# Block-sparse attention and a low-rank mixer with MLP: another order of the first loads and mask products, and other constants of the planner

## The chip, the core and the metric

The kernel runs on one core of a Trainium2 chip. The core has a matrix engine (TensorE, PE in the profile; its weight loads are shown as PEld), a vector engine (VectorE, DVE), a scalar engine for activation functions (ScalarE, ACT), a general-purpose engine (GpSimd, POOL) and an engine that mostly issues transfers (SyncE, SP). Each runs its own instructions in order, and they wait for each other on semaphores. ScalarE, SyncE and GpSimd also issue transfers (DMAs); all of them share 16 DMA engines.

The metric is the device time of one execution in microseconds (us). Smaller is better.

## What is computed

For 4 batches, 8 heads, 768 positions and a head width of 64, attention is taken under a mask of 24 x 24 blocks of 32 positions. The result, 768 x 512 per batch, is mixed along the positions by a product of rank 32, added to itself, and goes through a two-layer MLP of width 2048. Cut to its core:

```python
scores = scale * np.matmul(q, k.transpose(0, 1, 3, 2))
mask = np.abs(blk_i - blk_j) <= 1
mask = mask | (blk_i == 0) | (blk_j == 0) | (blk_i == n_blocks - 1) | (blk_j == n_blocks - 1)
for qb in range(n_blocks):
    for kb in sampled_blocks[qb]:
        mask[qb * 32:(qb + 1) * 32, kb * 32:(kb + 1) * 32] = True
scores = np.where(mask, scores, -1000000000.0)
attn = softmax(scores)
x = (attn @ v)                      # heads side by side: (B, S, 512)
u = x + (x.T @ U @ V).T             # rank 32, along the positions
out = u + np.maximum(u @ w_ch1, 0.0) @ w_ch2
```

Three random blocks per block row (sampled_blocks) come in as data; the rest of the mask is fixed and known when the program is built.

## The kernel before

**Tiling.** Two heads make a pair; there are 16 pairs, 4 per batch. A pair has 9 units. A unit is one tile of scores (psc, 128 keys x 512 queries for both heads, or two key tiles x 256 queries), two to four matmuls, one exponential of 128 x 1024 on ScalarE (est, line 497), and later its share of the value products (pav).

**Two stages.** In the first stage, pairs 0 to 3 run in a fixed order: scores of a unit, then the value products of the unit three before it, then side work listed in at_unit (line 983). Here the mask is added inside the score product: the upper or lower half of the rows of qa holds a mask row per query (0 or -240), and that of ka holds one-hot rows that pick the key's block. So the first scores need, for both heads, the turned (transposed) queries and keys and these extra rows. From the second stage on (pairs 4 to 15, batches 1 to 3) the mask is a product with 0/1 tiles m01 on VectorE (line 518), and the units are interleaved with the MLP of the batch before.

**The planner.** The order of the second stage is made when the program is built. A clock per engine (clk) is advanced by estimated costs, for example 0.92 us for an exponential and us=0.0315 for a value product (line 581). The MLP's steps lie in a list, fill, each with a cost: 0.65 us for a first-layer step (w1), 0.434 for a second-layer step (w2). Every fill step that is emitted adds its cost times a weight to a credit (line 1223: 0.87 for w1 steps, 1.13 for w2 steps). A unit that is due is emitted if the credit reaches rate() (line 1184), that is, the fill left less 12.5 us (14.5 in the last such batch), divided by the units left. It is also held back when ScalarE's clock is ahead of TensorE's by over 0.5 us (line 1195). If no fill step can go, a unit may go without credit. A first-layer or second-layer tile is made in two phases, which use the two halves of the array's rows crosswise; between them (the "swap" steps) 0.2 us must pass, which a unit may fill. Before the next batch's MLP opens, its last turned input (uT) must be there.

**The start.** The path to the first exponential is this:

- VectorE clears zeros, small, ka's extra rows, cbd, Ut and Vt (lines 286 to 292).
- SyncE loads sampled_blocks (sbi), then the queries in two parts (qld), the second part of the keys, and one set of one-hot rows. ScalarE's queue loads the first part of the keys (line 308), the fixed pattern (small, line 309, whose memory lies in w1t, which is its name in the profile), the identity id16 and the other set of one-hot rows. small has 24 rows: one-hot columns, the fixed mask, and block numbers.
- GpSimd writes ones into vt, then copies one element from kld into vld (line 321), which makes SyncE's load of v and all behind it wait for the first keys.
- TensorE runs eight products on zeros (warm_pe).
- VectorE compares block numbers with sbi (eq), reduces (cb) and joins the fixed mask (cbd), lines 336 to 359.
- TensorE makes three mask products (mask_mm: pm0 and pm1 for the first 512 queries of each head, pm2 for the other 256), one more warm product, turns four query tiles and two key tiles (turn_some, lines 410 and 411), and runs four more warm products.
- The first queries are cast by VectorE and the first keys by ScalarE (lines 403, 404). mask_rows turns pm0 and pm1 into extra rows of qa, on VectorE and ScalarE. half_copy puts the turned tiles into qa (VectorE) and ka (ScalarE).
- Then the first scores follow. pm2's rows and the rest of the turns follow after the first unit (lines 988 to 995).

Of the kernel before, what the change touches and what calls it, by code (L numbers as in the profile page):

```python
# [11 lines left out]
FP16 = mybir.dt.float16  # L12
# [5 lines left out]
P = 128  # L18
# [3 lines left out]
def kernel(  # L22
# [12 lines left out]
    nc = tc.nc  # L35

    B, H, S, D = q.shape
    BLK = 32
    NB = S // BLK
    T = S // P  # L40
# [7 lines left out]
    QA = 512  # L48
    QB = S - QA
# [16 lines left out]
    small_np = np.concatenate(  # L66
        [oh_np[:NB], ms_np, np.tile(np.arange(NB, dtype=np.float16), (NB, 1))], axis=1
    )
    eye16_np = np.eye(P, dtype=np.float16)

    small_dr = nc.inline_tensor(small_np, name="small_const")
# [6 lines left out]
    stpool = ctx.enter_context(tc.tile_pool(name="stpool", bufs=2))  # L78
# [19 lines left out]
    keep = tc.keep_in_program_order  # L98
# [5 lines left out]
    clk = {"pe": 0.0, "act": 0.0, "dve": 0.0, "pool": 0.0}  # L104
# [5 lines left out]
    def pst_tile(shape, dtype, name, tag):  # L110
        n = singles[tag][0]
        singles[tag].rotate(1)
        return psp[tag].tile(shape, dtype, tag=f"{tag}{n}", name=name)
# [58 lines left out]
    def mm(out, lhsT, rhs, start, stop, loose=False, us=0.0):  # L172
        clk["pe"] += us
        ins = nc.tensor.matmul(  # L174
            out, lhsT, rhs, start=start, stop=stop, skip_group_check=loose
        )
        keep(ins)
        return ins
# [25 lines left out]
    vts = [consts.tile([P, H, T, DV], FP16, name=f"vt{i}") for i in range(2)]  # L204
    Ut = wpool.tile([P, T, P], FP16)
    Vt = wpool.tile([P, T, P], FP16)
    Vd = wpool.tile([P, T, P], FP16)
    w1t = wpool.tile([P, NCC, CH], FP16)
    small = w1t[:, 0, 0 : S + 2 * NB]
    w2t = wpool.tile([P, NJJ, HD], FP16)  # L210

    rows = [slice(0, D), slice(D, P)]
# [12 lines left out]
    def new_ld(i, nm):  # L225
        lds[i, nm] = ldpool.tile([P, 2, T, D], FP32, tag="ld" + nm, name=nm + "ld")
        return lds[i, nm]
# [56 lines left out]


    keep(nc.vector.memset(zeros, 0.0))
    keep(nc.vector.memset(small, 0.0))
    for h in (1, 0):
        keep(nc.vector.memset(ka[0][h][mrows[h], :], 0.0))
    keep(nc.vector.memset(cbd, 0.0))  # L290
    keep(nc.vector.memset(Ut, 0.0))
    keep(nc.vector.memset(Vt, 0.0))
    qld, kld = new_ld(0, "q"), new_ld(0, "k")
    TQ, TK = 4, 2
    q0, k0 = src_of("q", 0), src_of("k", 0)

    def hot_rows(eng, st, h, n):
        r0 = mrows[h].start
        keep(eng.dma_start(out=ka[st][h][r0 : r0 + n, :], in_=oh_dr.ap()[0:n]))
# [3 lines left out]
            out=sbi[0:NB].rearrange("z r w -> z (r w)"),  # L303
            in_=sampled_blocks.bitcast(I32),
        )
    )
    keep(nc.sync.dma_start(out=qld[:, :, 0:TQ], in_=q0[:, :, 0:TQ]))
    keep(nc.scalar.dma_start(out=kld[:, :, 0:TK], in_=k0[:, :, 0:TK]))
    keep(nc.scalar.dma_start(out=small[0:NB], in_=small_dr.ap()))
    keep(nc.sync.dma_start(out=qld[:, :, TQ:T], in_=q0[:, :, TQ:T]))  # L310
    keep(nc.scalar.dma_start(out=id16, in_=eye16_dr.ap()))
    keep(nc.sync.dma_start(out=kld[:, :, TK:T], in_=k0[:, :, TK:T]))
    hot_rows(nc.scalar, 0, 0, NB)
    hot_rows(nc.sync, 0, 1, NB)
    keep(nc.scalar.activation(out=dummy, in_=zeros[:, 0:1], func=AF.Exp))


    for vt in vts:
        keep(nc.gpsimd.memset(vt[:, :, :, D : D + 1], 1.0))
    vld = new_ld(0, "v")  # L320
    keep(nc.gpsimd.tensor_copy(out=vld[:, 0, 0, 0:1], in_=kld[:, 0, 0, 0:1]))
    keep(nc.sync.dma_start(out=vld, in_=src_of("v", 0)))
# [4 lines left out]
    def warm_pe(n):  # L327
        for _ in range(n):
            mm(
                warm.rearrange("p (r n) -> p r n", r=4), zeros,  # L330
                zeros[:, None, :].broadcast_to([P, 4, P]), True, True,
            )

    warm_pe(8)

    keep(
        nc.vector.tensor_tensor(
            out=eq[0:NB],
# [7 lines left out]
            out=cb[0:NB],  # L346
            in_=eq[0:NB].rearrange("z r c -> z c r"),
# [6 lines left out]
            out=cbd[0:NB, :, 0:NB],  # L354
# [2 lines left out]
            op=ALU.max,  # L357
        )
    )
    qst = stpool.tile([P, T, 2, D], FP16, tag="stq", name="qst")  # L360
    kst = stpool.tile([P, T, 2, D], FP16, tag="stk", name="kst")

    def cast0(eng, st, ld, t0, t1):
        keep(
            eng(
                out=st.rearrange("p t h d -> p h t d")[:, :, t0:t1],
                in_=ld[:, :, t0:t1],
            )
        )


    def mask_mm(o, a, e):
        mm(
            o,
            cbd.rearrange("z a c -> z (a c)"),
            small[:, a:e],
            True, True,
        )

    def mask_rows(eng, h, i, a, e):  # L380
        o = qa[0][h][mrows[h], a:e]
        if eng == "dve":
            keep(
                nc.vector.tensor_scalar(
                    out=o, in0=i[mrows[h]],
                    scalar1=-MASK_BIAS, scalar2=MASK_BIAS, op0=ALU.mult, op1=ALU.add,
                )
            )
        else:
            keep(  # L390
                nc.scalar.activation(
                    out=o, in_=i[mrows[h]],
                    func=AF.Copy, scale=-MASK_BIAS, bias=MASK_BIAS,
                )
            )
# [3 lines left out]
    pm2 = pscp.tile([P, 2, 512], FP32, tag="double1", name="pm")  # L399
    mask_mm(pm0[:, 0, 0:QA], 0, QA)  # L400
    mask_mm(pm1, 0, QA)
    mask_mm(pm2[:, 0, 0:QB], QA, S)
    cast0(nc.vector.tensor_copy, qst, qld, 0, TQ)
    cast0(nc.scalar.copy, kst, kld, 0, TK)
    mask_rows("dve", 0, pm0[:, 0, 0:QA], 0, QA)
    mask_rows("act", 1, pm1, 0, QA)
    warm_pe(1)
    pq = pst_tile([P, T, P], FP16, "pturn", tag="ps")
    pk = pst_tile([P, T, P], FP16, "pturn", tag="ps")
    turn_some(qst, pq, 0, TQ)  # L410
    turn_some(kst, pk, 0, TK)
    warm_pe(4)

    def half_copy(eng, dst, h, pt, t0, t1):
        keep(
# [105 lines left out]
    def weights(ests, g, j, h):  # L521

        tr, kind = divmod(g, 2)
        if j < 4:
            return ests[3 * tr + kind][:, h, j * P : (j + 1) * P]
        return ests[3 * tr + 2][:, h, kind * QB + (j - 4) * P : kind * QB + (j - 3) * P]
# [42 lines left out]
    def values(i, ests, xs, xh, then):  # L569
        b, hp = divmod(i, HP)  # L570
        pav = double("pav")
        pv = pav[:, :, 0 : 6 * (D + 1)].rearrange("p c (m e) -> p c m e", e=D + 1)
        for c in range(2):
            for h in range(2):
                for j in range(3):
                    for g in range(T):
                        mm(
                            pv[:, c, 2 * j + h, :],
                            weights(ests, g, 3 * c + j, h),
                            vts[b % 2][:, 2 * hp + h, g, 0 : D + 1],  # L580
                            g == 0, g == T - 1, us=0.0315,
                        )

        def norm_both(eng):
            rcp = misc.tile([P, 2, 6], FP32, tag="rcp", name="rcp")
            keep(nc.vector.reciprocal(out=rcp, in_=pv[:, :, :, D]))  # L586
            keep(
                nc.vector.tensor_tensor(  # L588
                    out=xs.rearrange("p (c j) (h d) -> p c (j h) d", c=2, h=2),
                    in0=pv[:, :, :, 0:D],  # L590
                    in1=rcp[:, :, :, None].broadcast_to([P, 2, 6, D]),
                    op=ALU.mult,
                )
            )
            end = clk["dve"] + 1.17
            give_back(pav, end)
            keep(nc.gpsimd.tensor_copy(out=xh, in_=xs))  # L597
            then(run_on("pool", 1.15, end))
            return 1.17

        clk["pe"] += 0.2
        later("dve", 1, norm_both)
# [462 lines left out]
    fill = deque()  # L1065
# [78 lines left out]
    opened, credit = 1, 0.0  # L1144
# [39 lines left out]
    def rate():  # L1184

        left = sum(c for c, _, _ in fill)
        units = max(len(stream) - HP * NU * (B - 1 - opened), 0)
        if opened < B - 1:
            return max(left - 12.5, 0.0) / units if units else 1.2
        return max(left - 14.5, 0.0) / max(units, 1)  # L1190

    def try_unit(due):
        if not stream or state["out"] > 12 or not free_double():
            return False
        if clk["act"] > clk["pe"] + (0.5 if due else 1.0) or due and credit < rate():
            return False
        next_unit()
        return True
# [11 lines left out]
    while stream or fill or do_v or do_a or do_h or opened < B:  # L1210
        run_engines(clk["pe"])
        if not fill and opened < B and len(uT_at[opened]) == HP:
            if max(uT_at[opened]) <= clk["pe"]:
                fill.extend(mlp_steps(opened))
                opened += 1
        if try_h() or try_a() or try_values():
            continue
        if try_unit(True):
            credit -= rate()
            continue  # L1220
        if try_fill():

            weight = 0.87 if fill[0][0] > 0.5 else 1.13
            credit = min(credit + weight * run_fill(), 3.0)
            continue
        if try_unit(False):
            credit -= rate()
            continue
        clk["pe"] += 0.05
# [31 lines left out]
```

The softmax here doesn't subtract the row's maximum and nothing guards it: scores larger than these inputs give would overflow.

## Time and profile before

| | |
|---|---|
| time, median of 8 runs | 280.87 us (280.67 to 282.89) |
| profiled execution | 280.9 us, span of its instructions 279.1 us |
| TensorE busy | 272.3 us (98% of the span) |
| ScalarE busy | 176.9 us (63%) |
| VectorE busy | 175.3 us (63%) |
| GpSimd busy | 101.7 us (36%) |
| transfers | 31.71 MB, mean 114 GB/s |

[...] The shares are means over stages that have different limits. In the slices of the span, ScalarE is busy at nine tenths or more in the slices between about 7 and 42 us, and TensorE is busy at nine tenths or more in all slices but the first and the last. The costliest groups are the exponentials (144, 142.0 us), the first-layer products (896, 94.6 us), the second-layer products (688, 93.3 us) and the mask products with m01 on VectorE (108, 78.7 us).

In lines of the profile, "L174" is the helper mm, through which almost every matmul goes, so a matmul is told by what it writes. "<-" in brackets names what ended the wait before an instruction. The times in the first column of a timeline are counted from the span's start.

### The profile page before, as it was taken

The numbers are of one execution on the slowest core, as the hardware profiler recorded it, in microseconds if no ns is written. First come the engines' busy times: TensorE is split into PE (matmuls) and PEld (weight loads), VectorE is DVE, ScalarE is ACT, GpSimd is POOL, SyncE is SP. The second block draws the span as 40 slices with busy tenths as digits, with TensorE's granted clock in tenths as the row PEclk, the third lists the DMA queues.
The fourth block names the chain that finished last, engine by engine and source line by source line (L and its number), as shares of the span: only waits on it lengthen the run. The fifth ranks groups of instructions, "written<-read, shape, count | busy, mean of one in ns | idle before, by whom it ended". The sixth has DMA issues, their size and how long they took to land.

```text
span 279.1 us, 8049 instructions
## 1 busy us (share of the span) xinstructions
PE 272.3 (98%) x3497; PEld 162.6 (58%) x3497; DVE 175.3 (63%) x286; ACT 176.9 (63%) x199; POOL 101.7 (36%) x134
## 2 busy tenths in 40 slices
PE   8999999999999999999999999999999999999994
PEld 3577775565656565657664656657565545665443
DVE  5867758878798977865867576875879431000112
ACT  3999995869798947684956566794968002664000
POOL 2769549306384844353506454451102020000000
PEclk9999999999999999999999999999999999999999
DMA  6999956999979999996994999992100213000222
GB/s 187 305 321 245 286 131 91 176 178 117 116 50 128 140 131 150 159 88 77 74 98 31 164 83 159 154 109 46 31 2 18 89 36 140 7 0 2 75 75 78
DMA packets 85652, 31.71 MB, mean 114 GB/s; under 512 B 75304, under 2 KB 83216, under 8 KB 85616
## 3 DMA queue, kind: packets, MB, share of 16 engines
q0 software_dynamic: 49824, 10.29, 47.3%
q1 hardware_dynamic: 35304, 20.66, 35.5%
q8 instruction: 27, 0.44, 0.7%
q10 hardware_dynamic: 488, 0.24, 0.3%
q14 instruction: 9, 0.07, 0.1%
HBM read 27.90 MB, written 6.29 MB: 123 GB/s over the span
## 4 chain that ended last, share of the span: by engine, by line
PE 91%; ACT 3%; DVE 2%; POOL 1%; DMA 1%; issue 1%; DVEq 0%; ACTq 0%; POOLq 0%
PE pt L174 30%; PE pch L174 28%; PE psc L174 13%; PE pav L174 13%; ACT est L497 3%; PE pa L174 2%; PE ph L174 1%; POOL xh L597 1%; DMA w1t<-small_const 1%; PE pturn L267 1%; PE pmk L174 1%; PE warm L174 0%; PE pm L174 0%; PE puT L710 0%; DVE xh L540 0%
## 5 line engine op out<-in xcount | busy, mean ns | idle before, releaser
L497 ACT ACTIVATE est<-psc 128x1024 f16<-128x1024 f32 x144 | 142.0, 1028 | 38.7 <-PE psc L174 37.2
L174 PE MATMUL pt<-uT,w1t 64*128 64x384 f16 (+1 forms) x896 | 94.6, 324 | 0.5 <-ACT est L497 0.4
L174 PE MATMUL pch<-w2t,tT 64*128 64x512 f16 (+3 forms) x688 | 93.3, 372 | 0.2
L518 DVE TENSOR_TENSOR est<-est,m 128x1024 f16<-128x1024 f16 x108 | 78.7, 744 | 17.2 <-ACT est L497 16.0
L174 PEld LDWEIGHTS <-w1t 64*128 64x128 f16 (+1 forms) x896 | 46.7, 95 | 36.6 <-PE pt L174 6.8
L174 PEld LDWEIGHTS <-tT 64*128 64x128 f16 (+1 forms) x688 | 37.8, 95 | 38.5 <-PE pch L174 1.5
L735 ACT ACTIVATE tT<-pt 128x768 f16<-128x768 f32 (+1 forms) x48 | 36.8, 776 | 33.7 <-PE pt L174 33.7
L174 PEld LDWEIGHTS <-est 128*128 128x128 f16 x1152 | 41.4, 97 | 11.0 <-issue 5.1
L174 PE MATMUL pav<-vt,est 128*128 128x65 f16 x1152 | 44.5, 193 | 0.1
L790 DVE TENSOR_TENSOR of<-xf,pch 128x1024 f32<-128x1024 f32 (+3 forms) x16 | 15.2, 952 | 43.6 <-PE pch L174 43.5
L174 PE MATMUL psc<-qT,kT 64*128 64x512 f16 (+1 forms) x288 | 40.8, 323 | 0.0
L597 POOL CAST xh<-xs 128x768 f16<-128x768 f32 x12 | 11.4, 953 | 79.0 <-DVE xs L588 48.3
L683 POOL CAST uh<-xf 128x768 f16<-128x768 f32 x12 | 13.1, 1090 | 25.2 <-issue 12.9
L174 PE MATMUL psc<-qa,ka 128*128 128x512 f16 (+1 forms) x96 | 21.5, 326 | 0.2
L737 DVE TENSOR_SCALAR tT<-pt 128x768 f16<-128x768 f32 (+1 forms) x20 | 18.2, 915 | 4.7 <-PE pt L174 4.5
L174 PEld LDWEIGHTS <-kT 64*128 64x128 f16 x288 | 14.5, 94 | 11.0 <-DVE xs L588 0.2
L262 POOL DMA_DIRECT2D vt<-in_v_dram x20 | 16.3, 820 | 4.2 <-DMA w2t<-in_moe_w_ch_dram 4.2
L262 POOL DMA_DIRECT2D qst<-in_q_dram x20 | 16.3, 819 | 0.1
L262 POOL DMA_DIRECT2D kst<-in_k_dram x20 | 16.3, 820 | 0.0
L586 DVE RECIPROCAL rcp<-pav 128x12 f32<-128x12 f32 x12 | 2.8, 232 | 16.0 <-PE pav L174 16.0
L588 DVE TENSOR_TENSOR xs<-pav,rcp 128x768 f32<-128x768 f32 x12 | 11.5, 958 | 1.2
L674 DVE TENSOR_TENSOR xf<-xs,ph 128x768 f32<-128x768 f32 x12 | 11.4, 950 | 1.3 <-PE ph L174 1.3
(70 smaller groups left out, 137.3 us busy)
## 6 DMA issues: line engine op xcount, KB each, us to landing
out_dram<-of SPq DMA_DIRECT2D x9, 512.0 KB, 4.0
vld<-in_v_dram SPq DMA_DIRECT2D x6, 384.0 KB, 6.4
w1t<-in_moe_w_ch_dram POOLq DMA_DIRECT2D x4, 512.0 KB, 9.0
w2t<-in_moe_w_ch_dram POOLq DMA_DIRECT2D x4, 512.0 KB, 11.0
qld<-in_q_dram SPq DMA_DIRECT2D x5, 384.0 KB, 5.8
kld<-in_k_dram SPq DMA_DIRECT2D x5, 384.0 KB, 8.7
qst<-in_q_dram POOLq DMA_DIRECT2D x20, 96.0 KB, 4.0
kst<-in_k_dram POOLq DMA_DIRECT2D x20, 96.0 KB, 5.1
```

The costliest lines, as they stand in the source:

```text
L174: ins = nc.tensor.matmul(out, lhsT, rhs, start=start, stop=stop, skip_group_check=loose)
L262: keep(nc.gpsimd.dma_start(out=o[:, h], in_=src_of(nm, i)[:, h]))
L497: keep(nc.scalar.activation(out=est, in_=psc, func=AF.Exp, scale=0.125))
L518: keep(nc.vector.tensor_tensor(out=o, in0=o, in1=m, op=ALU.mult))
L586: keep(nc.vector.reciprocal(out=rcp, in_=pv[:, :, :, D]))
L588: nc.vector.tensor_tensor(out=xs.rearrange("p (c j) (h d) -> p c (j h) d", c=2, h=2), in0=pv[:, :, :, 0:D], in1=rcp[:, :, :, None].broadca ...
L597: keep(nc.gpsimd.tensor_copy(out=xh, in_=xs))
L674: nc.vector.tensor_tensor(out=u.rearrange("p (c j) n -> p c j n", c=2), in0=xs.rearrange("p (c j) n -> p c j n", c=2), in1=ph[:, :, 0:HS]. ...
L683: keep(nc.gpsimd.tensor_copy(out=uh, in_=u))
L735: keep(nc.scalar.activation(out=o, in_=i, func=AF.Relu))
L737: keep(nc.vector.tensor_scalar_max(out=o, in0=i, scalar1=0.0))
L790: nc.vector.tensor_add(out=of, in0=xfs[b][:, sc : sc + nsc, n0:n1], in1=pch)
```

## The change

The change has two groups of edits. The first is at the start. The pattern is padded from 24 to 32 rows, its memset is cut to the rows that the load doesn't write and put behind others, and its load goes ahead of the first keys on ScalarE's queue. Ut and Vt are cleared by GpSimd. The first keys are cast by GpSimd, in program order ahead of the copy that releases v's load. pm2 goes behind the turns, and the number of warm products ahead goes from 8 to 6, between products and turns from 1 to 0, and ahead of the scores from 4 to 2. The second group is five constants of the planner; they alter the order of the second stage and no instruction in it.

```diff
+    small_np = np.concatenate([small_np, np.zeros_like(small_np[: 32 - NB])])
...
     keep(nc.vector.memset(zeros, 0.0))
-    keep(nc.vector.memset(small, 0.0))
     for h in (1, 0):
         keep(nc.vector.memset(ka[0][h][mrows[h], :], 0.0))
     keep(nc.vector.memset(cbd, 0.0))
-    keep(nc.vector.memset(Ut, 0.0))
-    keep(nc.vector.memset(Vt, 0.0))
+    for r in (slice(32, 64), rows[1]):
+        keep(nc.vector.memset(small[r, 0:S], 0.0))
+    keep(nc.gpsimd.memset(Ut, 0.0))
+    keep(nc.gpsimd.memset(Vt, 0.0))
...
     keep(nc.sync.dma_start(out=qld[:, :, 0:TQ], in_=q0[:, :, 0:TQ]))
+    keep(nc.scalar.dma_start(out=small[0:32], in_=small_dr.ap()))
     keep(nc.scalar.dma_start(out=kld[:, :, 0:TK], in_=k0[:, :, 0:TK]))
-    keep(nc.scalar.dma_start(out=small[0:NB], in_=small_dr.ap()))
...
     for vt in vts:
         keep(nc.gpsimd.memset(vt[:, :, :, D : D + 1], 1.0))
+    cast0(nc.gpsimd.tensor_copy, kst, kld, 0, TK)
     vld = new_ld(0, "v")
     keep(nc.gpsimd.tensor_copy(out=vld[:, 0, 0, 0:1], in_=kld[:, 0, 0, 0:1]))
...
-    warm_pe(8)
+    warm_pe(6)
...
     mask_mm(pm0[:, 0, 0:QA], 0, QA)
     mask_mm(pm1, 0, QA)
-    mask_mm(pm2[:, 0, 0:QB], QA, S)
     cast0(nc.vector.tensor_copy, qst, qld, 0, TQ)
-    cast0(nc.scalar.copy, kst, kld, 0, TK)
     mask_rows("dve", 0, pm0[:, 0, 0:QA], 0, QA)
     mask_rows("act", 1, pm1, 0, QA)
-    warm_pe(1)
     pq = pst_tile([P, T, P], FP16, "pturn", tag="ps")
     pk = pst_tile([P, T, P], FP16, "pturn", tag="ps")
     turn_some(qst, pq, 0, TQ)
     turn_some(kst, pk, 0, TK)
-    warm_pe(4)
+    mask_mm(pm2[:, 0, 0:QB], QA, S)
+    warm_pe(2)
...
-                            g == 0, g == T - 1, us=0.0315,
+                            g == 0, g == T - 1, us=0.0331,
...
-            return max(left - 12.5, 0.0) / units if units else 1.2
-        return max(left - 14.5, 0.0) / max(units, 1)
+            return max(left - 11.0, 0.0) / units if units else 1.2
+        return max(left - 12.9, 0.0) / max(units, 1)
...
-        if clk["act"] > clk["pe"] + (0.5 if due else 1.0) or due and credit < rate():
+        if clk["act"] > clk["pe"] + (0.36 if due else 1.0) or due and credit < rate():
...
-            weight = 0.87 if fill[0][0] > 0.5 else 1.13
+            weight = 0.87 if fill[0][0] > 0.5 else 1.24
```

More of the change, by code (lines that the diff above doesn't have):

```diff
@@ L319, with cast0 @@
         keep(nc.gpsimd.memset(vt[:, :, :, D : D + 1], 1.0))
+    qst = stpool.tile([P, T, 2, D], FP16, tag="stq", name="qst")
+    kst = stpool.tile([P, T, 2, D], FP16, tag="stk", name="kst")
+    def cast0(eng, st, ld, t0, t1):
+        keep(
+            eng(
+                out=st.rearrange("p t h d -> p h t d")[:, :, t0:t1],
+                in_=ld[:, :, t0:t1],
+            )
+        )
+    cast0(nc.gpsimd.tensor_copy, kst, kld, 0, TK)
     vld = new_ld(0, "v")
@@ L359 @@
     )
[L360 to L369, printed above, removed]
     def mask_mm(o, a, e):
```

## The prediction

> **What bounds the kernel.** I read the busy time by stage first, then the start of the timeline, then the chain of waits.
>
> The first view is the busy time of the engines by stretch (PE, PEld, DVE, ACT, POOL, then clock, DMA share, GB/s):
>
> ```profile
> 8.00:16.00 8.00, 7.79 (x96) 5.11 (x94) 6.16 (x14) 7.65 (x9) 5.28 (x8) 1.00 1.07 294
> 24.00:32.00 8.00, 7.97 (x126) 6.08 (x124) 6.28 (x14) 7.99 (x10) 4.92 (x10) 1.00 1.05 269
> 114.00:142.00 28.00, 28.00 (x409) 17.23 (x406) 20.89 (x30) 22.20 (x26) 13.23 (x16) 1.00 1.33 98
> 205.00:234.00 29.00, 28.87 (x395) 15.46 (x392) 15.53 (x23) 8.35 (x9) 3.65 (x4) 1.00 0.17 52
> ```
>
> From 8 to 41 us ScalarE is full (7.99 of 8.00): 36 exponentials follow each other every 0.92 us. Later TensorE is full. So whatever starts the first exponential earlier moves everything behind it, and pacing can win only gaps of TensorE.
>
> The second view is the timeline of the first 9 us (start, duration, then in brackets the idle time before it and who ended that):
>
> ```profile
> 0.99 3.59 PE L174 MATMUL warm<-m 128*128 128x512 f16 x8 [0.99 <-DVE m L286]
> 1.40 0.55 ACTq L309 DMA_DIRECT2D w1t<-small_const  x1
> 1.98 0.35 ACTq L311 DMA_DIRECT2D id<-eye_const  x1
> 4.14 0.22 DVE L337 TENSOR_TENSOR eq<-w1t,sbi 24x72 f16<-24x72 f16 x1 [0.86 <-DMA w1t<-small_const]
> 4.75 0.41 DVE L365 CAST qst<-qld 128x512 f16<-128x512 f32 x1
> 4.88 1.25 PE L174 MATMUL pm<-w1t,cbd 128*128 128x512 f16 x3 [0.29 <-DVE cbd L353]
> 5.52 0.69 DVE L384 TENSOR_SCALAR qa<-pm 64x512 f16<-64x512 f32 x1 [0.36 <-PE pm L174]
> 6.34 0.45 PE L267 MATMUL pturn<-id,qst 128*128 128x128 f16 x4
> 6.75 1.03 PE L174 MATMUL warm<-m 128*128 128x512 f16 x4
> 6.83 0.88 DVE L416 COPY qa<-pturn 64x512 f16<-64x512 f16 x2 [0.62 <-PE pturn L267]
> 6.95 0.76 ACT L416 COPY ka<-pturn 64x256 f16<-64x256 f16 x2 [0.41 <-PE pturn L267]
> 7.61 0.59 PE L174 MATMUL psc<-qa,ka 128*128 128x512 f16 x2
> ```
>
> The pattern (named w1t, whose memory it borrows) lands at 4.02; three small VectorE steps give cbd at 4.82; three mask products and one warm matmul stand ahead of the turns at 6.34; copies and four warm matmuls end near 7.7; the second score matmul starts at 7.82 and the first exponential at 8.24. A matmul of 512 columns takes 0.43 us up to 4.58 and 0.22 at 6.75: the array runs at half rate until about 6.45 (the clock column shows 1.00 there too, so the spacing tells it).
>
> The third view is the chain of waits:
>
> ```profile
> 55.02 2.86 ACT est L497 x3
> 57.93 0.83 PE pt L174 x8
> 66.68 1.03 ACT est L497
> 233.90 20.91 PE pt L174 x128
> 254.80 20.77 PE pch L174 x112
> ```
>
> After 233.9 nothing but matmuls at full rate is left (20.91/128 = 0.163 us). Between 48 and 234 I added up the starts of matmuls that come more than 0.06 us after their predecessor's columns are through: 3.9 us, of which fifteen times 0.1 are the switch to the value products. Some 2.3 us are open to pacing, the largest 0.52 at 57.93, behind the three exponentials.
>
> **Start: the pattern.** Its load loses the wait for a memset (0.97 to 1.37) and goes from second to first on ScalarE's queue: issued at 0.74. The key load, issued at 0.74 now, lands at 2.98 with 128 KB; the pattern has 51 KB, so 2.3 to 3.0. VectorE's list before it is 0.11 + 2 x 0.38 + 0.11 + 2 x 0.38 us with its gaps: free at 2.8 (3.28 now; one 0.38 memset changed for two, two given away). eq, cb, cbd take 4.14 to 4.82, 0.68 us: cbd at 3.5 to 3.75, products from 3.55 to 3.8, two at 0.43 done by 4.4 to 4.65. That is over 1.1 us earlier, but what is late next is what the turns read: the identity (issued 1.98, landed 5.03) and the query part (landed 4.41, cast 0.41 on a VectorE that is now waiting: 4.86). So the turns start at about 5.1 instead of 6.34, and TensorE idles 0.45 to 0.7 us ahead of them.
>
> [...] By the row, 2.62 us from issue to landing becomes 2.24 or less through the place in the queue alone. I count nothing for the padding; being wrong by 0.3 us costs nothing, since the identity is later.
>
> **Start: the turns.** Six turns at half rate, 0.107 apart: q done 5.64, k done 5.85. The third mask product (0.21) and two warm matmuls (0.43) follow: TensorE free at 6.65 (rate doubling at 6.45) to 6.81. VectorE: cast to 4.86, mask rows 0.69 to 5.58, q copies 0.88 from 5.70: 6.58. ScalarE: table load and dummy end at 4.9 as now, mask rows 0.59 to 5.5, k copies 0.76 from 5.9: 6.66. The second score matmul then stands at 6.8 to 7.05 and the exponential 0.42 later, at 7.25 to 7.5: against 8.24 a gain of 0.75 to 1.0; I take **0.85**.
>
> **Start: what else is moved.** The first key load goes from first to second on its queue (issue 1.3, landing 3.5 to 4.2 instead of 2.98). Its cast moves to GpSimd: 0.54 us by the 256-column cast there, against 0.39 on ScalarE; ahead of it two memsets of 384 words (between 0.3, as the shorter vt memset, and 0.85, as a cast of 768; I take 0.5 each). Done by 4.8, needed at 5.5. Behind it on GpSimd stands the touch of vld that lets SyncE load v, at about 4.8 instead of 3.29, and SyncE's three loads of pair 1 behind that. v (landed 8.38, cast from 9.06, first value product 10.83) can slip to about 8.8 before it costs. This delay also helps: the one-hot rows of the first keys, 36 KB each, land only at 7.20 and 7.53, since v's 384 KB run among them. Needed bytes still open at 4.41 are 128 + 32 + 256 + 72 = 488 KB; at the 143 + 204 KB moved by 6.0 and 335 GB/s behind that, 6.4. If they stayed at 7.53, the second score matmul would stand at 7.62 and the gain be 0.2.
>
> **Does it carry on?** ScalarE's gaps between 8.24 and 45.41 sum to 0.33 us, and the next loads have at least 1.5 us before their turns (pair 1's keys land 10.55, turned 13.93). So the 0.85 is kept.
>
> **The pacing.** Units issued follow from rate(): left units fall as (left fill - c) to the power of the weight. Batch 0: 39.0 us of fill, 33 units: with c = 12.5 and 0.87 some 21 go into the w1 part, with 11.0 some 20. Batch 1: 16 becomes 15.5. Batch 2 (c 14.5 to 12.9): 17.3 becomes 16.6. The trace has 17 and 18 exponentials in those two stretches, so the formula holds. A unit costs TensorE 0.22 us wherever it stands; in w1 it also fills one of 16 swaps between row halves, which stand open for some 0.23 us without it. So half a unit less costs about 0.1 us a batch; against it, fewer units and the limit 0.36 (from 0.5) when ScalarE is behind spare the gap at 57.93 and that at 67.75 (0.52 + 0.23). The value products' 0.0331 is what the trace has (2.38/72), a correction of 0.12 us a pair in the plan. Net I take **0.25** gained; bounds: 1.5 gained if most of the 2.3 goes, 1.5 lost if a handover between batches comes late.
>
> **Sum.** 0.85 + 0.25 = 1.1 us. The profiled execution took 280.9 (span 279.1 and 1.8 around it), the median is 280.87: **279.8**. About 0.84 us (0.3%) is what can be told from no change: faster is below 280.03, slower above 281.71.
>
> **Rivals.**
> - *The clock (slower).* [...] Chance 0.10.
> - *A late handover (slower).* Units end 1.5 us nearer the end of the fill. Batch 0's last turn is issued 108.18 and batch 1 starts 114.22, some 2 us after it landed; a turn that waits on SyncE behind a key's would leave TensorE idle 2 us: 281.8. Chance 0.10.
> - *The one-hot rows stay late:* gain 0.2 and pacing 0.1: 280.5. Chance 0.13.
> - *Pacing takes most gaps:* 1.3 more: 278.6. Chance 0.12.
> - The forecast, 279.3 to 280.4: 0.55; about four fifths of it is below 280.03.
>
> Faster: 0.43 + 0.12 = 0.55. Within 0.3%: 0.12 + 0.13 + 0.05 = 0.30. Slower: 0.15. The range, 278.8 to 281.6, leaves out half of the clock's and the handover's cases and a part of the best.
>
> **What would show it.** First exponential at 7.25 to 7.5; turns at 5.1, ended by the identity; eq at 2.8 to 3.1; no 512-column matmul at 0.43 after 7; first out-projection (pch) and the stage end at 233.9 earlier by about 1.1. It is wrong if the first exponential stays beyond 7.9, if the 36 exponentials show gaps, or if pt begins a batch after a wait for uT.

## The result and the profile after

| | before | changed |
|---|---|---|
| median | 281.05 us (56 runs) | 280.18 us (19 runs) |
| runs | 280.34 to 282.89 | 278.75 to 281.22 |
| ratio to before | | 0.9962, 95% interval 0.9951 to 0.9973 |
| profiled execution (span) | 280.9 (279.1) | 280.3 (278.5) |

By the ratio, the change makes the kernel faster by 0.38%, some 1.1 us (the two medians differ by 0.87). The forecast was 1.1. But the profile says that they do not come from where the forecast put them.

The timeline of the changed kernel's start (start, duration, instruction, idle time before it and who ended it):

```profile
0.74 0.38 ACTq L310 DMA_DIRECT2D w1t<-small_const  x1
3.06 0.22 DVE L351 TENSOR_TENSOR eq<-w1t,sbi 24x72 f16<-24x72 f16 x1
3.80 1.03 PE L175 MATMUL pm<-w1t,cbd 128*128 128x512 f16 x2
5.57 0.38 PE L268 MATMUL pturn<-id,qst 128*128 128x128 f16 x4 [0.74 <-DMA id<-eye_const]
6.52 0.78 PE L175 MATMUL psc<-qa,ka 128*128 128x512 f16 x2
7.34 3.87 ACT L498 ACTIVATE est<-psc 128x1024 f16<-128x1024 f32 x4 [0.48 <-PE psc L175]
```

The pattern's products start at 3.80 instead of 4.88, the turns wait for the identity, and the first exponential starts at 7.34 instead of 8.24: 0.90 us won. What follows is new. TensorE's timeline at the key turns of pair 1:

```profile
12.79 0.40 PE L175 MATMUL pav<-vt,est 128*128 128x65 f16 x8
14.69 0.51 PE L268 MATMUL pturn<-id,kst 128*128 128x128 f16 x6 [1.50 <-POOL kst L249]
```

TensorE stands still for 1.5 us and waits for a cast on GpSimd. GpSimd's own timeline tells why:

```profile
4.95 0.40 POOL L325 CAST kst<-kld 128x256 f16<-128x256 f32 x1 [2.34 <-DMA kld<-in_k_dram]
5.29 0.19 POOL L335 COPY vld<-kld 128x1 f32<-128x1 f32 x1
...
13.81 0.83 POOL L249 CAST kst<-kld 128x768 f16<-128x768 f32 x1 [3.19 <-DMA kld<-in_k_dram]
```

The first keys land only at 4.89. The copy at 5.29 releases v's load and all loads behind it on SyncE. In the kernel before, this copy and the cast of pair 1's keys stood here:

```profile
3.04 0.19 POOL L321 COPY vld<-kld 128x1 f32<-128x1 f32 x1 [1.78 <-DMA kld<-in_k_dram]
10.60 0.83 POOL L248 CAST kst<-kld 128x768 f16<-128x768 f32 x1
```

So v's load is issued at 5.50 (3.29 before), the load of pair 1's keys at 6.43 (4.83 before), and these keys land at 13.75 (10.55 before). The DMA share from 5 to 9 us, in forty slices of 0.1 us, shows the hole, first in the changed kernel:

```profile
DMA  6999863211000005682389999999999899999999
```

and in the kernel before:

```profile
DMA  9494359798799999878989999999899797988998
```

From 5.7 to 6.5 us the DMA engines of the changed kernel have almost nothing to do (share 0.07 and 26 GB/s, against 1.03 and 316 before). Then the delay doubles: 1.6 us at the issue of pair 1's keys are 3.2 us at their landing. From 9 to 11 us, with these keys under way, the engines move 174 GB/s where they moved 342 before; why is not shown. The busy time by stretch (PE, PEld, DVE, ACT, POOL, clock, DMA share, GB/s) shows what that costs:

```profile
8.00:16.00 8.00, 6.40 (x77) 4.12 (x76) 5.03 (x11) 6.49 (x8) 3.29 (x5) 1.00 1.02 261
13.00:15.00 2.00, 0.50 (x13) 0.38 (x10) 0.00 (x0) 1.23 (x2) 0.83 (x1) 1.00 1.09 249
```

and in the kernel before:

```profile
13.00:15.00 2.00, 2.00 (x36) 1.52 (x34) 1.41 (x3) 2.00 (x3) 0.43 (x2) 1.00 1.10 351
```

ScalarE, the pacer of this stage, is busy 6.49 of the first 8 us instead of 7.65. The rest is in the chain of waits, in order of time:

```profile
57.38 0.43 PE psc L175 x6
57.82 1.30 PE pt L175 x16
...
68.20 1.03 ACT est L498
...
233.64 20.91 PE pt L175 x128
```

Before, 2.86 us of exponentials lay on the chain from 55.02, and TensorE had its largest gap after them. Here that stretch is matmuls without a gap. Behind it, VectorE's and GpSimd's steps on the value products (63.97 to 66.74) and one exponential, at 68.20, lie on the chain.

I cut each profiled execution at four points: the first exponential, the first first-layer product (pt), the first of the 128 closing pt, and the end of the span. The last column is when the trace's record of the full clock begins.

| kernel | first exp. | to pt | pt to closing | rest | full rate from |
|---|---|---|---|---|---|
| before | 8.24 | 36.93 | 188.66 | 45.26 | 6.47 |
| changed | 7.34 | 38.97 | 187.26 | 44.93 | 5.11 |
| difference | -0.90 | +2.04 | -1.40 | -0.33 | |

The sum is -0.59, the difference of the spans. So the start wins 0.9 and loses 2.0 right after, the pacing brings 1.4, and 0.3 come at the end. One profile is one execution; the experiments are there to tell how much of this holds in the median.

The third stretch shows where the pacing's gain lies. I took the time from the end of a product's columns (at 0.163 us for 384) to the start of the next product, and counted what is over 0.15 us. Before there are eight such gaps of TensorE, 2.28 us in all; in the changed kernel there are three, 0.94 us. The difference, 1.34, is nearly all of the 1.40: 0.54 of it stood behind exponentials, 0.34 behind the cast of xh on GpSimd, and 0.46 at swaps between row halves that no unit filled.

### The profile page after: what moved, and what is told of

The parts are those of the page before. It is cut to its first block, busy times and chain, and to the rows that moved or that the text cites. A ratio compares the mean times of both kernels' runs of the same rounds, so it can differ in the third digit from the quotient of the medians.

```text
span 278.5 us, 8037 instructions
## 1 busy us (share of the span) xinstructions
PE 270.3 (97%) x3492; PEld 161.5 (58%) x3492; DVE 174.9 (63%) x285; ACT 177.2 (64%) x198; POOL 103.0 (37%) x137
## 4 chain that ended last, share of the span: by engine, by line
PE 90%; DMA 5%; DVE 2%; POOL 1%; ACT 1%; issue 0%; ACTq 0%; SPq 0%; POOLq 0%; DVEq 0%
PE pch L175 30%; PE pt L175 30%; PE pav L175 13%; PE psc L175 12%; DMA qld<-in_q_dram 3%; PE pa L175 2%; DMA id<-eye_const 1%; PE ph L175 1%; PE pturn L268 1%; ACT est L498 1%; POOL xh L598 0%; PE puT L711 0%; DVE xh L541 0%; DVE xs L589 0%; PE pmk L175 0%
## 5 line engine op out<-in xcount | busy, mean ns | idle before, releaser
L175 PEld LDWEIGHTS <-w1t 64*128 64x128 f16 (+1 forms) x896 | 46.0, 95 | 36.2 <-PE pt L175 8.4
L598 POOL CAST xh<-xs 128x768 f16<-128x768 f32 x12 | 10.4, 870 | 79.5 <-DVE xs L589 73.9
L684 POOL CAST uh<-xf 128x768 f16<-128x768 f32 x12 | 13.9, 1161 | 26.1 <-DVE xf L675 14.5
L589 DVE TENSOR_TENSOR xs<-pav,rcp 128x768 f32<-128x768 f32 x12 | 11.5, 958 | 1.2
L175 PEld LDWEIGHTS <-ka 128*128 128x128 f16 (+1 forms) x108 | 8.6, 97 | 3.5 <-issue 1.6
## 6 DMA issues: line engine op xcount, KB each, us to landing
w2t<-in_moe_w_ch_dram POOLq DMA_DIRECT2D x4, 512.0 KB, 10.2
```

The lines of the kernel that those rows point to most:

```text
L175: ins = nc.tensor.matmul(out, lhsT, rhs, start=start, stop=stop, skip_group_check=loose)
L589: nc.vector.tensor_tensor(out=xs.rearrange("p (c j) (h d) -> p c (j h) d", c=2, h=2), in0=pv[:, :, :, 0:D], in1=rcp[:, :, :, None].broadca ...
L684: keep(nc.gpsimd.tensor_copy(out=uh, in_=u))
```

## Experiments

All kernels in one table (as above; the ratio is that to the kernel before, with its interval):

| | median | ratio | first exp. | to pt | pt to closing | rest | full rate |
|---|---|---|---|---|---|---|---|
| e1 | 279.77 | 0.9956 (0.9936 to 0.9975) | 9.65 | 36.94 | 187.27 | 45.27 | 8.76 |
| e2 | 281.32 | 1.0000 (0.9984 to 1.0016) | 7.27 | 37.78 | 188.65 | 44.92 | 4.17 |
| e3 | 279.85 | 0.9942 (0.9920 to 0.9964) | 8.65 | 37.17 | 187.27 | 44.91 | 9.32 |
| e4 | 279.87 | 0.9940 (0.9918 to 0.9962) | 7.50 | 37.35 | 187.21 | 44.94 | 4.08 |
| p1 | one run | | 8.18 | 37.45 | 188.62 | 45.30 | 5.57 |
| p2 | one run | | 7.96 | 36.93 | 188.03 | 45.30 | 5.93 |
| p3 | one run | | 8.06 | 36.95 | 188.76 | 45.29 | 5.85 |
| p4 | one run | | 8.31 | 36.95 | 188.09 | 45.30 | 6.39 |
| e5 | 279.78 | 0.9952 (0.9935 to 0.9969) | 8.21 | 37.69 | 187.26 | 44.94 | 10.11 |
| e6 | 279.61 | 0.9941 (0.9926 to 0.9957) | 7.44 | 38.96 | 187.26 | 44.91 | 5.85 |
| e7 | 278.78 | 0.9930 (0.9910 to 0.9950) | 7.48 | 36.94 | 187.25 | 44.93 | 5.78 |
| e8 | 279.67 | 0.9945 (0.9919 to 0.9971) | 7.45 | 38.07 | 187.63 | 44.94 | 5.05 |

The third stretch is the same within 0.06 us in all kernels with the same five constants, whatever their start (187.21 to 187.27), so one run is enough to compare it. The first two vary between executions of the same start. A row's profile need not be typical of its median: the profiled run of e1 took 280.92, that of e2 280.40 and that of e4 278.77, each about 1 us from its median, and that of e7 (278.38) was the fastest of six.

### Which half brings the gain: e1 and e2

e1 is the kernel before with the five new constants; e2 is the changed kernel with the five old ones.

> The kernel before with the five constants of the planner alone. Theory A (the start gains 0.9 us at the first exponential and gives some 2 us back while pair 1 and pair 2 wait for loads; pacing then wins back 1.4 us or more): 1.3 to 1.8 us faster than before, near 279.4; the first exponential stays at 8.2 us and the 128 closing first-layer products start near 232.4. Rival B (as in the prediction: the start keeps its gain and pacing brings 0.25): 0.1 to 0.5 us faster, near 280.7.

> The changed kernel with the old five constants. Theory A: 0.5 to 1.3 us slower than before, near 281.9; first exponential near 7.35, then TensorE idle 1 to 1.6 us ahead of pair 1's key turns. Rival B: 0.8 us faster, near 280.1, no such wait beyond 0.3 us in most profiles (the one of the changed kernel was an accident of the transfers).

The constants alone give 0.9956, all that the change gives (0.9962). The start alone gives 1.0000. So rival B falls: its 0.3% for the start lies outside e2's interval, its 280.7 for the pacing (0.999) outside e1's. Theory A has the place right, but the loss of the start in the median is about as large as its gain, not larger. In e2's profile it is 0.85 of 0.97. TensorE's timeline of e2 has the same wait, shorter:

```profile
13.70 0.51 PE L268 MATMUL pturn<-id,kst 128*128 128x128 f16 x6 [0.57 <-POOL kst L249]
```

But ten of e2's 22 runs lie at 280.1 to 281.0 and twelve at 281.2 to 282.7, and this profile is of one of the ten (280.40). So what takes the gain in the median may be more than this wait; the next profile has a candidate.

e1's profile missed in one point: its first exponential comes at 9.65, not 8.2, with the very start of the kernel before. Its TensorE timeline:

```profile
5.45 1.25 PE L174 MATMUL pm<-w1t,cbd 128*128 128x512 f16 x3 [0.87 <-DVE cbd L353]
7.56 1.63 PE L174 MATMUL warm<-m 128*128 128x512 f16 x4
9.02 0.59 PE L174 MATMUL psc<-qa,ka 128*128 128x512 f16 x2
```

The pattern landed later in this execution, so the mask products start 0.57 us later and TensorE's gap ahead of them is 0.87 us, not 0.29. And four warm products take 1.63 us where they took 1.03: the array still runs at half rate. When it doubles differs between executions of the same start (8.76 here, 6.47 before); together the two make the first exponential 1.4 us later here.

### Why pair 1's loads are late: e3, e4 and e5

e3 puts the first keys ahead of the pattern again; e4 also moves the copy that releases v's load ahead of the cast:

```diff
-    keep(nc.scalar.dma_start(out=small[0:32], in_=small_dr.ap()))
     keep(nc.scalar.dma_start(out=kld[:, :, 0:TK], in_=k0[:, :, 0:TK]))
+    keep(nc.scalar.dma_start(out=small[0:32], in_=small_dr.ap()))
...
-    cast0(nc.gpsimd.tensor_copy, kst, kld, 0, TK)
     vld = new_ld(0, "v")
     keep(nc.gpsimd.tensor_copy(out=vld[:, 0, 0, 0:1], in_=kld[:, 0, 0, 0:1]))
+    cast0(nc.gpsimd.tensor_copy, kst, kld, 0, TK)
```

e5 keeps the changed order of the loads, and the copy reads the pattern:

```diff
-    cast0(nc.gpsimd.tensor_copy, kst, kld, 0, TK)
     vld = new_ld(0, "v")
-    keep(nc.gpsimd.tensor_copy(out=vld[:, 0, 0, 0:1], in_=kld[:, 0, 0, 0:1]))
+    keep(nc.gpsimd.tensor_copy(out=vld[:, 0, 0, 0:1], in_=small[:, 0:1]))
+    cast0(nc.gpsimd.tensor_copy, kst, kld, 0, TK)
```

> The changed kernel with the first keys ahead of the pattern on ScalarE's queue again (the pattern still needs no memset). Theory A (what delays the later loads is that the first keys land at 4.89 instead of 2.98, and the copy that releases v's load waits for them): keys land near 3.0, v's load is issued near 3.7 instead of 5.5, pair 1's keys land by 11.5, the wait ahead of their turns is under 0.4 us, first exponential stays under 7.6; about 1.2 to 1.9 us faster than the changed kernel, near 278.6. Rival B (late landing comes from the copies of qa and the one-hot rows for the second buffer, which share the DMA engines at that time): pair 1's keys still land after 13, time as the changed kernel, 280.2.

> As e3, and the one-element copy that releases v's load stands ahead of the cast of the first keys on GpSimd. Theory A: v's load is issued near 3.3, 0.4 us earlier than in e3; pair 1's loads land about 0.3 us earlier; but v's bytes run among the one-hot rows again, which then land at 7.0 to 7.5 and hold the first exponential at 7.7 to 8.1. Net 0 to 0.5 us slower than e3, near 279. If the one-hot rows don't follow v's load, the first exponential stays at 7.4 and the time equals e3's.

> The changed kernel with the one-element copy that releases v's load reading the pattern (landed 2.57) instead of the first keys (landed 4.89), and ahead of their cast on GpSimd. Theory A (the start's gain is lost because v's load, and pair 1's loads behind it, are held until 5.5, while the DMA engines run dry at 6.0 to 6.6 us): v's load is issued before 3.4, no slice of the DMA share under 0.5 between 5 and 9 us, pair 1's keys land by 11.5 and their turns wait under 0.3 us; the one-hot rows and the identity land later, first exponential 7.4 to 8.2; 0.8 to 1.5 us faster than the changed kernel, near 279.0. Rival B (pair 1's keys are late for another reason): they land after 13, time as the changed kernel.

In all three v's load is issued at 3.35 to 3.56, and the wait ahead of pair 1's key turns is gone. The cast of these keys starts at 10.2 (e3), 11.1 (e4) and 12.4 us (e5). Over all profiles it starts at 12.8, 13.8 and 14.1 in the three kernels that hold v's load beyond 5 us (e2, changed, e6), and at 10.2 to 12.4 in the eleven others. So the late release is shown as the cause of the wait, and rival B falls (the copies of qa are in all of them). But single executions scatter by 2 us, and e5's keys landed later than said (12.38, not by 11.5). The gain over the changed kernel, 0.1 to 0.2% of the time, is within the intervals: said was 0.3 to 0.7%.

The profiles show two things that may have eaten it. In e3 and e4 the pattern is late again; VectorE in e4:

```profile
4.27 0.22 DVE L351 TENSOR_TENSOR eq<-w1t,sbi 24x72 f16<-24x72 f16 x1 [1.25 <-DMA w1t<-small_const]
```

Freed of its memset but second in the queue, it lands at about 4.2. In e4, whose rate doubled early (4.08), the first exponential still comes at 7.50, only 0.16 later than in the changed kernel. And in e3 and e5 the array doubled late (9.32 and 10.11). TensorE in e5:

```profile
7.06 1.12 PE L175 MATMUL psc<-qa,ka 128*128 128x512 f16 x2
7.97 0.63 PE L175 MATMUL warm<-m 128*128 128x512 f16 x1
```

The warm product of 0.63 us, 0.38 in the changed kernel's profile, is one at half rate; with it first exponentials came at 8.65 and 8.21, and e5's second one 0.9 us late (10.13). In e5 the rate is not alone in this: the last one-hot rows landed at 7.45 (6.58 in the changed kernel), and the second score product starts at 7.59.

### The gap ahead of the turns: e6 and e7

e6 is the changed kernel with two more warm products; e7 adds e5's edit.

```diff
     mask_rows("act", 1, pm1, 0, QA)
+    warm_pe(2)
     pq = pst_tile([P, T, P], FP16, "pturn", tag="ps")
```

> The changed kernel with two more warm products between the mask products and the turns, where TensorE stands idle 0.7 to 1 us. Theory A (the rate of TensorE doubles only after a window without such a gap, so that in some executions the first scores still run at half rate): the doubling comes before 7.9 in the profile and the slowest executions go: median 0.2 to 0.5 us under the changed kernel's, its spread of 2.5 us becomes narrower. Rival B (one gap of this size doesn't matter): median as the changed kernel or 0.1 to 0.4 slower, since the turns stand behind 0.86 us of products at half rate.

> e5 and e6 together. Theory A: both gains, 278.7 to 279.0, and executions within 1.5 us of each other. Rival B: as the better of the two.

e7's TensorE and its GpSimd:

```profile
4.62 1.06 PE L175 MATMUL warm<-m 128*128 128x512 f16 x2
5.47 0.54 PE L268 MATMUL pturn<-id,qst 128*128 128x128 f16 x4
...
6.58 0.86 PE L175 MATMUL psc<-qa,ka 128*128 128x512 f16 x2
```

```profile
3.09 0.24 POOL L332 CAST vld<-w1t 128x1 f32<-128x1 f16 x1 [0.48 <-DVE w1t L292]
...
10.75 0.83 POOL L249 CAST kst<-kld 128x768 f16<-128x768 f32 x1 [0.56 <-DMA kld<-in_k_dram]
```

The fill costs the turns nothing: they start at 5.47, and at 5.57 in the changed kernel, where the identity (landed 5.53) held them. And pair 1's keys are cast in time. In this profile both parts of the start's gain are kept: 7.48, and 36.94 to the first pt. e7 has the lowest median here, 278.78 us, 0.9930 of before. Its interval (to 0.9950) lies just under that of the changed kernel (from 0.9951), but it overlaps those of e5 and e6, and it has six runs, 1.6 us apart. By the ratios, e5 gains 0.1% on the changed kernel, e6 0.2% and e7 0.3%, as theory A said; no step between e5, e6 and e7 is clear of noise. Nor does an early release always keep the gain: e8 has the same start, and its profile takes 38.07 to the first pt, with a wait of 0.90 us on ScalarE for pair 2's queries.

In the three profiles with the fill the rate doubles at 5.05, 5.78 and 5.85. In the five with a gap and the new order it doubles at 4.08, 4.17, 5.11, 9.32 and 10.11, the first three of them before the gap's end. Eight of the fourteen profiles have the doubling behind a gap of TensorE, ahead of the mask products or the turns. With gaps of 0.26 to 0.54 us (before and p1 to p4) it comes at 5.57 to 6.47; with gaps of 0.58, 0.87 and 1.29 us (e5, e1, e3) at 8.76 to 10.11. So among these eight the three with a gap over 0.55 us are the late ones, as theory A of e6 has it. Eight executions don't prove that the gap is the cause, and what sets the moment of the doubling is not shown.

e6 has a median 0.2% under the changed kernel's, with overlapping intervals, and its runs are not closer together (278.38 to 282.34; without the slowest, to 280.36), so that part of the expectation missed. Its profile keeps the wait of 1.61 us on ScalarE for pair 1's keys.

### Which constants: p1 to p4, and e8

Each is the kernel before with one edit of the five (p2 has both ends of rate()); e8 is e7 with the weight back at 1.13.

```diff
p1  -us=0.0315          +us=0.0331
p2  -left - 12.5, 14.5  +left - 11.0, 12.9
p3  -else 1.13          +else 1.24
p4  -(0.5 if due        +(0.36 if due
```

> The kernel before with the value products' planned cost alone changed (0.0315 to 0.0331). Read from the profile alone: the stretch from the first first-layer product (pt) to the first of the 128 closing ones, 188.66 us before and 187.27 with all five constants, the same within 0.05 us in every profile so far. Theory A (the win comes from the plan's shares of units and from holding units back when ScalarE is behind): 188.4 to 188.7. Rival B (the win is a plan whose clock of TensorE is right): under 187.8.

> The kernel before with the two ends of rate() alone changed (12.5 to 11.0, 14.5 to 12.9). The same stretch. Theory A: 188.0 to 188.4, since fewer units fall into batch 0's first layer, where ScalarE is behind. Rival B: 188.6 or more, since the last turn of a batch comes nearer to the next one.

> The kernel before with the weight of second-layer steps alone changed (1.13 to 1.24). The same stretch. Theory A: 188.3 to 188.6 (the weight acts on second-layer stretches, where gaps of TensorE were 1.2 us in all, two of 0.31 behind the cast of xh). Rival B: 188.7 or more, for a unit there comes earlier and fills no swap.

> The kernel before with the limit on ScalarE's lag alone changed (0.5 to 0.36). The same stretch. Theory A: 187.8 to 188.1, the gap of 0.52 us at 57.93 behind three exponentials and one of 0.23 go. Rival B: 188.5 to 188.7, the units held back leave swaps open that cost as much.

> e7 with the weight of second-layer steps back at 1.13. Alone it lengthened the stretch from the first first-layer product to the closing ones by 0.10 us (p3), and the four single changes sum to 1.14 us where all five constants together bring 1.40. Theory A (the edits add up; the weight is no part of the win): the stretch takes 187.1 to 187.2, time as e7's, 278.7. Rival B (the weight pays only beside the others): 187.4 to 187.7 and 0.2 to 0.4 us slower than e7. In either case the start as in e7: doubling of TensorE's rate before 8 us, first exponential under 8.2, no wait over 0.3 us ahead of pair 1's key turns.

Against 188.66 the stretch becomes shorter by 0.04 (p1, within the scatter of 0.06), 0.63 (p2) and 0.57 (p4), and longer by 0.10 (p3). p1, p2 and p4 lie where theory A put them, p3 where its rival did. But p2's reason was wrong: batch 0's first layer holds 19 exponentials as before. The chain of waits of p4, where before three exponentials stood:

```profile
56.32 0.43 PE psc L174 x6
56.75 1.30 PE pt L174 x16
```

and of p2:

```profile
62.07 1.03 ACT est L497
63.10 0.04 issue
63.15 0.83 PE pt L174 x8
```

In p4 the run of matmuls goes through; in p2 one exponential is left, later, where three and then one more (66.68) stood. Both take ScalarE off the path, by different edits. Nor is p3's loss the open swaps that its rival named. The two gaps of 0.31 us behind the cast of xh (148.48 and 163.26 before) are gone, as theory A said. But TensorE has two new gaps: 0.38 us at 93.45, where scores wait for the transposed keys (kT), and 0.26 us at 115.08, behind an exponential.

The four sum to 1.14, all five give 1.40. e8 tells where the difference is: without the new weight, the stretch is 187.63, 0.38 longer. The longest gap that it has and e7 has not is one of 0.28 us at 197.84, behind an exponential. So the weight costs 0.10 alone and pays 0.38 beside the others, as rival B said. e8's median is 0.9 us over e7's, but it comes from another series, in which the kernel before had 280.83 and not 281.12; by the ratios the difference is some 0.4 us, with overlapping intervals.

## Why the prediction was right, and where it was not

- **Sum.** 279.8 was said, 1.1 us faster; measured 280.18, by the ratio 1.1 us faster. The number is right by luck, because two errors cancel: the start kept nothing in the median where 0.85 was counted, and the pacing brought 1.40 where 0.25 was counted. The 0.33 us at the program's end had no term at all. One mark was missed: the closing products were to start 1.1 us earlier, and start 0.26 earlier (233.57) in the profile.
- **Start, the pattern.** Landed 2.57 (said 2.3 to 3.0), eq at 3.06, products at 3.80: right, at the late end (VectorE was free at 3.03; the memsets named make 2.9, not the 2.8 of the sum). The load's landing is told by 12 semaphore updates before (3.73 to 4.02) and by 16 after (2.41 to 2.57); whether the padding buys time was not tried alone. Right, too, was what is late next, the identity. It landed at 5.53, not 5.03, half a microsecond after what was taken over from before.
- **Start, the turns.** The score matmul at 6.92 and the exponential at 7.34 lie in the ranges. The late identity was made up by a rate that doubled at 5.11 in this execution, so the six turns took a half of what was counted (0.055 us apart, not 0.107).
- **Start, one-hot rows.** They landed at 5.88 and 6.58 (said 6.4), so that rival did not happen. The reason given, v's load running among them, is not all of it: with v's load issued early again the last of them land at 6.6 to 6.9 in e4, e7 and e8, and only in e5 at 7.45.
- **"Does it carry on?" is the step that failed.** It took over pair 1's landing (10.55) and its slack from the trace of before, although the paragraph ahead of it had v's load and SyncE's three loads move 1.5 us. The first keys landed at 4.89 (said 3.5 to 4.2), v's load was issued 2.2 us later and that of pair 1's keys 1.6 us later; these keys landed 3.2 us later, and the DMA engines had run dry in between. The slack from landing to turn (10.55 to 13.93) also had to hold the cast of 0.83 us and turns that could go 0.7 us earlier (13.19, where TensorE begins to wait). So the 36 exponentials do show gaps, which was named as a sign of being wrong. e2 shows the price: the start is worth 0 in the median, not 0.85. e7's profile shows that the loss is not a part of the gain. What remains open is how much of the median's loss is the loads' and how much the late doubling's: e5, with the loads mended, and e6, with the gap filled, each gain 0.1 to 0.2% on the changed kernel, within the intervals.
- **The pacing** had its place right (gaps of TensorE, the largest at 57.93, bound 1.5) and its size wrong: 0.25 was said, 1.40 measured. The term that was mis-sized is what a held-back unit and a later end spare: 0.57 and 0.63. It was netted against swaps left open, but fewer stand open: three gaps of 0.22 us before (77.74, 222.59, 230.27), one after. And of the eight gaps only two, 0.52 and 0.23 us, were counted as spared; the other six, 1.5 us, were put at nothing. The count of units had an error as well: it was held to be confirmed by 17 and 18 exponentials (16 and 17 by the formula), but for batch 0 the formula gave 21, where the trace has 19. The truer cost of value products in the plan brings 0.04.
- **The clock rival.** Its chance of 0.10, and its share in the 0.15 for slower and in the range, was the author's estimate: no run shows what makes the rate double late. What the runs show is that it can, and what that costs. With doubling at 9.32, e3's first exponential comes 1.15 us later than that of e4 (8.65 against 7.50), whose pattern is as late and whose rate doubled at 4.08; with doubling at 10.11, e5's second exponential comes 1.8 us later than in the changed kernel (10.13 against 8.35). But e1 shows a late doubling with the old start too (8.76, first exponential at 9.65), behind a gap of 0.87 us, so it is no mark of the change alone. How often it comes is not known: one run of each kernel was profiled.
- **The late handover** did not appear: no batch's first pt waits for uT in the changed kernel's chain.

## What to carry to other kernels

Where an edit delays an instruction that releases a queue, follow every transfer behind it to its consumer before a gain is called kept; slack read from the old trace holds only for the old issue times. A one-element copy that paces loads should hang on the first thing that lands, not on a load that the same edit moves back. When a planner's constants change, size the win by the gaps on the chain that they can remove and try each constant beside the others, since one that costs alone can pay in company.

## What was not expected of the hardware

- The array's rate doubled between 4.08 and 10.11 us after the span's start, in kernels whose first matmuls start at the same 0.99. This moves the first exponential by about 1 us (8.65 in e3, 7.50 in e4), and may be one source of the 2.5 us between runs of the changed kernel.
- The rest after the first closing product is 45.26 to 45.30 us in the six kernels with the old start and 44.91 to 44.94 in the eight with the new one, with the same matmuls. The 0.33 us lie after the last store, between two semaphore instructions of GpSimd at the program's end: 0.36 us before (278.02 to 278.38) and 0.06 after (277.78 to 277.84). What takes the time there stays open.
- Clearing 128x768 f16 takes GpSimd 0.74 us; the same tile took VectorE 0.38.
